# Packed attention and a gated feed-forward in one kernel: two weight loads moved ahead, two output chunks begun within h of batch 0, one packed product on its own

## The chip, the cores and the metric

The kernel runs on one core of a Trainium2 chip. The time is that of the device, in microseconds (us), for one execution; three executions were timed, and their median is the figure. A profile is one further execution, recorded instruction by instruction; it has its own time.

The engines are named as the profile names them: PE is TensorE (matmuls; PEld its weight loads), DVE is VectorE, ACT is ScalarE, POOL is GpSimd (here it mostly issues loads), SP is SyncE (it issues stores and transposes by DMA). Each engine works through its own instructions in order.

## The reference

```python
def sm_attn(qq, kk, vv):
    s = scale * np.matmul(qq, kk.transpose(0, 1, 3, 2))
    s = s - np.max(s, axis=-1, keepdims=True)
    a = np.exp(s)
    a = a / (np.sum(a, axis=-1, keepdims=True) + 1e-09)
    return np.matmul(a, vv)
p_packed = sm_attn(p, k, v)
out = sm_attn(q, p_packed, p_packed)
...
x = np.ascontiguousarray(attn_out.transpose(0, 2, 1, 3)).reshape(B * S, H * D)
...
h = x @ w_in
g = h * np.cos(h)
return (g @ w_out).astype(np.float32)
```

There are 8 batches, 8 heads, 576 tokens and 64 elements a head, with 32 packed queries p a head; w_in is 512 x 2048 and w_out 2048 x 512. All inputs are float32.

## The kernel before

**Stages of a batch b.** `s1(b)`: scores of the packed queries against the keys, and their exp. `a1_pe` or `a1_xbar`: that exp transposed, on TensorE or by a DMA that SP issues. `pp(b)` (line 191): the packed product, exp times values, 48 small matmuls. `pp_T(b)`: its transpose, `ppT`. `ppw(b, n)` (line 213): packed product times quarter n of w_in, into `PPW[b]`; so the second attention and x @ w_in become one product. `s2(b)`, `sums2(b, y)`, `normalise(b)`: exp of the queries' scores against the packed product, their sums, and the normalised weights `a2n`. Then h, in 16 chunks of 128 columns: two or four matmuls of `PPW` and `a2n`, a cosine on ScalarE into `cosT` (a pool of three buffers), and h times cosine on VectorE into `gT`. Last the output: `gT` times `w_out`, in chunks of 128 tokens by 16 matmuls of 512 columns each, copied out of PSUM and stored by SP. 576 tokens are four and a half chunks; the halves of two batches go together in `joint`, chunk 4 of every odd batch.

For batches 0 and 1 a chunk of h has 512 tokens in one PSUM bank (`h_one`, line 295), and `h_half` (line 310) does the last 64 tokens of eight chunks in one bank. Later batches use `h_mm` (line 268), 576 tokens over a pair of banks.

**The filler.** Output matmuls are queued (`set_filler(b)` appends those of batch b) and `fill(n)` issues the next n of them wherever it stands, so that TensorE has work between dependent steps. Those of batch 0 come from `out_first` (line 370), in an order of its own: four chunks are open at once, 0 and 1 in the pool `O` of two banks, 2 and 3 in the pool `psX`. Its tuples are (chunk, up to which of 16).

**PSUM banks.** Beside `O` there are six banks, arranged anew by `banks(kind)`: as three pairs (`psa()` takes them in turn), or as six single ones H0 to H5 (`one()` takes them in turn by `turn[0]`), or with two of them held for `psX`. A bank is written again only after the last reader of what it held.

**The order of the work is written out by hand.** Lines 420 to 517 are the start: the loads, all issued by POOL in the order of the text, attention of batch 0, h of batch 0 (lines 478 to 489), `ppw` of batch 1 for n of 0 to 2 (lines 492 to 497), then the query transposes, `s2`, `sums2` and `normalise` of batch 1. POOL has eight load slots in turn: a load is issued only when the one eight before it has landed. From line 519 on, `slot(s, ...)` runs the 16 chunks of h of batch s. It spreads the output matmuls left in the filler over the chunks by `weight` or `heavy`; `hooks` are (chunk, function) pairs that put other steps in between; with `trail`, the output of batch s itself is appended at chunk 10 and its first `trail` matmuls are issued in the slot; `keep` leaves some for later. `last` is called within chunk 15. In slot 1 the hooks hold the half chunks of batches 0 and 1, the fourth `ppw` of batch 1 and work for batch 2. In slots 2 to 6 the hook is `tiled(s)` (line 540): two `ppw` of batch s and `pp` of batch s+1 in one go, the latter into unused columns of a chunk's bank. Between slots, lines 577 to 610 and 613 to 643 do the attention of the next batches, with fills.

Of the kernel before, what the change touches and what calls it, by code (L numbers as in the profile page):

```python
# [15 lines left out]
def kernel(  # L16
# [143 lines left out]
    def s1(b):  # L160
        ps = scores(lambda r, h, e: P2[r, b, h, :], xT["k", b])
        sm = small.tile([128, 2], FP32, name="sums1")
        for y in range(2):
            ACT.activation(  # L164
                out=a1[b % 2][:, y, :, 0:TP].rearrange("p (e m) x -> p e m x", e=2),
                in_=ps[y][:, :, 0:HS].rearrange("p e (m x) -> p e m x", m=3),
                func=AF.Exp, scale=scale, accum_out=sm[:, y:y + 1])
        sums1[b] = sm
# [22 lines left out]
    def pp(b, eng=V, own=None):  # L191

        ps = own() if own else psa()[:, 0, :]
        for y in range(2):
            for j in range(C):
                c = 2 * (j % 3) + j // 3
                for x in range(4):
                    nc.tensor.matmul(ps[32 * x:32 * x + 32, y * D:(y + 1) * D],  # L198
                                     a1T[b][0:TP, y, j, 32 * x:32 * x + 32],
                                     bf["v", b][:, 2 * x + y, c * D:(c + 1) * D],  # L200
                                     start=(j == 0), stop=(j == C - 1))
        t = pp_sb[b % 2].rearrange("p a d -> p (a d)")
        copy(eng, t[:, 0:2 * D], ps[:, 0:2 * D])
        copy(eng, t[:, 2 * D:3 * D], ps[:, 0:D])

    def pp_T(b, eng=V, own=None):
        ps = own(BF16) if own else psa(BF16)[:, 0, :]
        t = pp_sb[b % 2].rearrange("p a d -> p (a d)")
        for i in range(2):
            nc.tensor.transpose(ps[:, i * 128:(i + 1) * 128], t[:, i * D:i * D + 128], ident)  # L210
        copy(eng, ppT[b % 2].rearrange("p i x n -> p (i x n)"), ps[:, 0:256])

    def ppw(b, n, eng=None, own=None, later=False, cuts=((0, 512),)):
        if b not in PPW:
            PPW[b] = ppw_pool.tile([128, 2, DF], BF16, name="PPW", tag="PPW")
        two = isinstance(eng, tuple)
        if own:
            ps = [own(), own()]
        else:
            t = psa()  # L220
            ps = [t[:, 0, :], t[:, 1, :]]
        for x in range(4):
            for y in range(2):
                r = slice(64 * y, 64 * y + 64)
                nc.tensor.matmul(ps[y][32 * x:32 * x + 32, :], ppT[b % 2][r, 0, x, :],  # L225
                                 w_in_bf[r, x, n * 512:(n + 1) * 512], start=True, stop=True)

        def evacuate(cuts=cuts):
            if own or two:
                for a, z in cuts:  # L230
                    for y in range(2):
                        copy(eng[y] if two else eng, PPW[b][:, y, n * 512 + a:n * 512 + z], ps[y][:, a:z])
            else:
                copy(eng or (V, ACT)[n % 2], PPW[b][:, :, n * 512:(n + 1) * 512], t)
        if later:
            return [lambda c=c: evacuate((c,)) for c in cuts]
        evacuate()
# [131 lines left out]

    def out_first():  # L370

        pss = {}
        for c, fcs in ((0, 4), (1, 4), (2, 4), (3, 4), (0, 8), (1, 8), (2, 8), (3, 8),
                       (2, 12), (3, 12), (2, 16), (3, 16), (0, 16), (1, 16)):
            if c not in pss:
                pss[c] = (O if c < 2 else psum["psX"]).tile([128, DM], FP32, name="ot", tag="ot")
            for fc in range(8 if (c, fcs) in ((0, 16), (1, 16)) else fcs - 4, fcs):
                nc.tensor.matmul(pss[c], gT[0][:, fc, c * 128:(c + 1) * 128], w_out_bf[:, fc, :],  # L378
                                 start=(fc == 0), stop=(fc == NFC - 1))
                if fc == NFC - 1:  # L380
                    store(0, c, pss[c], V if c == 2 else ACT)
                    if c == 3:
                        banks("single")
                        turn[0] = 3
                yield

    filler = []

# [14 lines left out]
    def load_w_in(n):  # L403
        G.dma_start(out=w_in_bf[:, :, n * 512:(n + 1) * 512],
                    in_=moe_w_in.rearrange("(a p) n -> p a n", p=128)[:, :, n * 512:(n + 1) * 512])

    def load_w_out(n):
        G.dma_start(out=w_out_bf[:, n * 4:(n + 1) * 4, :],
                    in_=moe_w_out.rearrange("(a p) n -> p a n", p=128)[:, n * 4:(n + 1) * 4, :])
# [32 lines left out]
    warm(1, None, wz4)  # L442
    pe_T("k", 0, (V, ACT, V))
    s1(0)
    load_w_in(3)
    load("v", 1)
    warm(1, None, wz4, 192)
# [4 lines left out]
    warm(1)  # L452
    pp_T(0)
    pe_T("q", 0, (V, ACT, V))
    load_w_out(0)
    load("q", 1)
    for n in range(1, 4):
        load_w_out(n)
    G.dma_start(out=p_raw[:, 4:, :], in_=p_rows[:, 4:, :])
    load("k", 2)  # L460
# [14 lines left out]
    banks("single")  # L475
    a1_pe(1, own=one)
    recips(1)
    for fc in range(13):
        h_one(0, fc)()()
        if fc in (0, 4, 8):  # L480
            ppw(0, 1 + fc // 4, (ACT, ACT if fc == 8 else V), own=bank)
    c13 = h_one(0, 13)
    pp(1, ACT, own=bank)
    c13()()
    c14 = h_one(0, 14)
    c15 = h_one(0, 15)
    pp_T(1, ACT, own=bank)
    c14()()
    c15()()
    set_filler(0)  # L490
    fill(4)
    for n, at in ((0, 2), (1, 0), (2, 4)):
        turn[0] = at
        if n == 2:
            fill(4)
            ACT.preload_act_table_set(EXP_SET)
        ppw(1, n, (ACT, V), own=one)
    banks("held")
    t = psa(BF16)
    for i in range(2):  # L500
# [10 lines left out]
    sums2(1, 0)  # L511
    fill(2)
    sums2(1, 1)
    fill(9)
    normalise(1)
    ACT.preload_act_table_set(SIN_SET)
    fill(4)

    def slot(s, hooks, keep=0, heavy={}, last=None, trail=0, weight=None):

        left, done = to_do() - keep + trail, 0
        weight = weight or [1 + heavy.get(fc, (0, 0))[0] for fc in range(NFC)]
        for fc in range(NFC):
            rest = h_one(s, fc)() if s == 1 else h_mm(s, fc)
            if fc == NFC - 1 and last:
                last()
            rest()
            if fc == 10 and trail:  # L530
                set_filler(s)
            quota = (left * sum(weight[:fc + 1])) // sum(weight) - done
            done += quota
            behind = min(quota, heavy[fc][1]) if fc in heavy else quota
            fill(quota - behind)
            while hooks and hooks[0][0] == fc:
                hooks.pop(0)[1]()
            fill(behind)
# [19 lines left out]
    def cross(n, b):  # L558
# [1 line left out]

    osb_eng[0] = ACT
    banks("four")
    slot(1, [(5, lambda: h_half(0, 0)), (6, cross("k", 3)), (6, lambda: h_half(0, 1)),
             (7, lambda: ppw(1, 3, (ACT, V), own=one)), (9, cross("q", 2)), (9, lambda: h_half(1, 0)),
             (10, lambda: pack_p(2, 4, one(BF16))), (11, lambda: h_half(1, 1)), (12, tk2),
             (13, lambda: pe_T("k", 2, (None, None, V), (2,), own=one))],
         trail=8, heavy={5: (0, 1), 6: (0, 1), 7: (0, 1), 9: (0, 1), 11: (0, 1)},
         weight=[3, 3, 3, 4, 4, 2, 2, 2, 3, 2, 2, 2, 1, 2, 3, 3])
    banks("pairs")
    ACT.preload_act_table_set(EXP_SET)  # L570
    osb_eng[0] = V
# [36 lines left out]
        load(n, b)  # L608
    fill(9)
    osb_eng[0] = ACT  # L610
    slot(2, [(7, lambda: tiled(2))], 0, {7: (6, 4)}, lambda: pp_T(3, V))

    for s in range(3, B):
        nxt = s + 1 < B
        ACT.preload_act_table_set(EXP_SET)
        osb_eng[0] = V
        if s % 2:
            set_filler(s - 1)
        fill(5)
        s2(s)  # L620
        ppw(s, 0, V)
        fill(8 if nxt else 9)
        if nxt:
            s1(s + 1)
            ppw(s, 1, V)
            a1_xbar(s + 1)
            xbar("q", s + 1)
            recips(s + 1)
            if s + 2 < B:
                xbar("k", s + 2)  # L630
                behind(xT["k", s + 2][0:1, 0, 0:1])
        else:
            for n in range(1, 4):
                ppw(s, n, V)
        fill(4 if nxt else 5)
        sums2(s, 0)
        fill(5)
        sums2(s, 1)
        normalise(s)
        ACT.preload_act_table_set(SIN_SET)  # L640
        fill(13)
        osb_eng[0] = ACT
        for n, b in (("v", s + 2), ("q", s + 2), ("k", s + 3)):
            if b < B:
                load(n, b)
        if nxt:
            slot(s, [(7, lambda: tiled(s))], 0 if s % 2 else 1, {7: (5, 4)}, lambda: pp_T(s + 1, V),
                 7 if s % 2 else 0)
        else:
            slot(s, [], trail=7)  # L650
    fill(1000)
    tail_chunk(B - 1, 4)

# [29 lines left out]
```

## Time and profile before

| what | value |
|---|---|
| median of three runs | 243.86 us (243.74 to 244.26) |
| the profiled execution | 244.22 us, of which the span of the instructions is 242.4 us |
| granted TensorE clock | 0.999 of full |
| matmuls | 2244 |
| idle time of the TensorE rows from 36 to 234 us | 0.6 us |
| w_in's quarters, from issue to landing | 14.3 to 19.7 us, median 17.0 |
| w_out's quarters, from issue to landing | 20.8 to 21.5 us, median 21.1 |
| costliest group: output matmuls, 448 of 128x512 | 114.8 us busy |
| h matmuls of batches 2 to 7, 384 of 128x288 | 62.7 us busy |
| h times cosine on VectorE, 96 of 128x576 | 71.4 us busy, mean 757 ns |

How to read it: a row of the timeline has its start, its length in us, the engine, the line, what it writes and reads, how many instructions were merged into it, and in brackets how long the engine was idle before it and what ended that. Matmuls overlap, so a row's length is longer than the time until the next can start, and idle time in a TensorE row is less than what TensorE really waited. A row of the stretches has, after the stretch and its length, the busy time and count of PE, PEld, DVE, ACT and POOL, then the granted clock, the DMA share and GB/s.

### The profile page before, as it was taken

How to read it: one execution, taken by the hardware profiler on the slowest of the kernel's cores; microseconds unless marked ns; L12 is line 12 of the kernel's file. 1: busy time of each engine (PE TensorE's matmuls, PEld its weight loads, DVE VectorE, ACT ScalarE, POOL GpSimd, SP SyncE). 2: the span in 40 equal slices, each digit the busy share in tenths (PEclk: the TensorE clock that was granted, in tenths of full speed). 3: DMA queues.
4: the chain of work that ended last, by engine and by line, in shares of the span. 5: the costliest groups of instructions: out<-in, count | busy, mean ns of one | idle time of the engine just before them, and what ended most of it. 6: DMA issues, size and time to landing. Idle time of an engine off the chain costs nothing.

```text
span 242.4 us, 5480 instructions
## 1 busy us (share of the span) xinstructions
PE 232.9 (96%) x2244; PEld 126.0 (52%) x2244; DVE 162.8 (67%) x261; ACT 166.5 (69%) x268; POOL 36.2 (15%) x58
## 2 busy tenths in 40 slices
PE   7789899999999999999999999999999999999994
PEld 3454244456445564556546554556456554565453
DVE  3259993688558786687857686777758787877001
ACT  2349899688659778876878677867787683776110
POOL 8522212200300005000500311030100110010000
PEclk9999999999999999999999999999999999999999
DMA  6999999999999999999999999989285101311133
GB/s 96 203 205 206 206 206 225 201 235 201 175 133 162 197 183 166 211 179 179 186 209 225 184 191 208 191 160 213 66 161 119 46 0 46 87 43 46 47 83 87
DMA packets 64376, 37.37 MB, mean 154 GB/s; under 512 B 36864, under 2 KB 59776, under 8 KB 64352
## 3 DMA queue, kind: packets, MB, share of 16 engines
q0 software_dynamic: 23152, 18.75, 51.7%
q1 hardware_dynamic: 40960, 18.16, 37.1%
q8 instruction: 17, 0.28, 0.5%
q10 hardware_dynamic: 240, 0.13, 0.2%
q14 instruction: 7, 0.06, 0.1%
HBM read 37.22 MB, written 9.44 MB: 192 GB/s over the span
## 4 chain that ended last, share of the span: by engine, by line
PE 83%; DMA 8%; DVE 4%; ACT 2%; issue 1%; POOLq 0%
PE ot L365 42%; PE psA L275 17%; PE ot L378 6%; DMA a1T<-a 5%; PE psH L301 4%; DMA kbf<-in_k_dram 3%; PE psA L155 2%; PE psA L225 2%; PE psA L251 2%; PE psA L198 1%; PE ot L348 1%; DVE gT L307 1%; DVE PPW L96 1%; PE psA L128 1%; PE psH L316 1%; DVE a2n L261 1%
## 5 line engine op out<-in xcount | busy, mean ns | idle before, releaser
L365 PE MATMUL ot<-w_out_bf,gT 128*128 128x512 bf16 x448 | 114.8, 379 | 0.0
L282 DVE TENSOR_TENSOR gT<-psA,cosT 128x576 bf16<-128x576 f32 x96 | 71.4, 757 | 16.3 <-ACT cosT L279 15.3
L279 ACT ACTIVATE cosT<-psA 128x576 bf16<-128x576 f32 x96 | 62.4, 652 | 21.3 <-PE psA L275 20.0
L275 PE MATMUL psA<-a2n,PPW 128*128 128x288 bf16 x384 | 62.7, 286 | 0.0
L365 PEld LDWEIGHTS <-gT 128*128 128x128 bf16 x448 | 42.1, 98 | 38.2 <-issue 4.2
L275 PEld LDWEIGHTS <-PPW 128*128 128x128 bf16 x384 | 37.5, 98 | 25.4 <-issue 0.6
L96 DVE CAST PPW<-psA 128x1024 bf16<-128x1024 f32 x19 | 23.0, 1220 | 7.9 <-PE psA L225 7.9
L307 DVE TENSOR_TENSOR gT<-psH,cosT 128x512 bf16<-128x512 f32 x32 | 21.0, 688 | 4.5 <-ACT cosT L306 4.4
L96 DVE COPY osb<-ot 128x512 f32<-128x512 f32 (+2 forms) x18 | 11.7, 649 | 16.1 <-PE ot L348 14.6
L306 ACT ACTIVATE cosT<-psH 128x512 bf16<-128x512 f32 x32 | 18.5, 615 | 4.6 <-PE psH L301 3.5
L94 ACT COPY osb<-ot 128x512 f32<-128x512 f32 (+1 forms) x20 | 11.4, 568 | 14.8 <-PE ot L365 12.2
L261 DVE SCALAR_TENSOR_TENSOR a2n<-a2u,r,lns 128x576 bf16<-128x576 bf16 x16 | 12.4, 815 | 12.4 <-ACT lns L259 12.4
L301 PE MATMUL psH<-a2n,PPW 128*128 128x512 bf16 x64 | 17.7, 380 | 1.0 <-DVE PPW L96 1.0
L378 PE MATMUL ot<-w_out_bf,gT 128*128 128x512 bf16 x64 | 17.8, 380 | 0.1
L286 POOL COPY joint<-gT 128x512 bf16<-128x512 bf16 x12 | 7.3, 616 | 64.6 <-DVE gT L282 64.6
L164 ACT ACTIVATE a<-psA 128x576 bf16<-128x576 f32 x16 | 10.3, 646 | 7.8 <-PE psA L155 7.8
L253 ACT ACTIVATE lns<-psA 128x576 f32<-128x576 f32 x16 | 10.4, 651 | 7.4 <-PE psA L251 6.8
L365 PE MATMUL ot<-w_out_bf,joint 128*128 128x512 bf16 x48 | 14.6, 379 | 0.0
L243 ACT ACTIVATE a2u<-psA,rs 128x576 bf16<-128x576 f32 x16 | 11.0, 737 | 1.4 <-PE psA L155 1.4
L109 POOL COPY gate<-kT 1x1 bf16<-1x1 bf16 x4 | 0.7, 178 | 74.4 <-DMA kT<-kbf 74.4
L301 PEld LDWEIGHTS <-PPW 128*128 128x128 bf16 x64 | 5.8, 98 | 8.3 <-DVE PPW L96 2.0
L259 ACT ACTIVATE lns<-lns 128x576 f32<-128x576 f32 x16 | 10.0, 673 | 0.0
(94 smaller groups left out, 197.0 us busy)
## 6 DMA issues: line engine op xcount, KB each, us to landing
kbf<-in_k_dram POOLq DMA_DIRECT2D x8, 576.0 KB, 14.6
vbf<-in_v_dram POOLq DMA_DIRECT2D x8, 576.0 KB, 8.7
qbf<-in_q_dram POOLq DMA_DIRECT2D x8, 576.0 KB, 11.5
out_dram<-osb SPq DMA_DIRECT2D x24, 192.0 KB, 2.8
out_dram<-osb SPq DMA_DIRECT2D x22, 128.0 KB, 2.5
w_in_bf<-in_moe_w_in_dram POOLq DMA_DIRECT2D x4, 512.0 KB, 17.0
w_out_bf<-in_moe_w_out_dram POOLq DMA_DIRECT2D x4, 512.0 KB, 21.1
out_dram<-osb SPq DMA_DIRECT2D x25, 64.0 KB, 2.7
```

The lines of the kernel that those rows point to most:

```text
L94: ACT.copy(out=out, in_=in_)
L96: eng.tensor_copy(out=out, in_=in_)
L243: ACT.activation(out=a2u[b][:, y].rearrange("p (e x) -> p e x", e=2), in_=ps[y][:, :, 0:HS], func=AF.Exp, scale=rs1[b][:, y:y + 1])
L261: V.scalar_tensor_tensor(out=a2n[b][:, y], in0=a2u[b][:, y], scalar=r1[b][:, y:y + 1], in1=lns[b][:, y], op0=ALU.mult, op1=ALU.mult)
L275: nc.tensor.matmul(ps[:, e, 0:HS], PPW[b][:, y, fc * 128:(fc + 1) * 128], a2n[b][:, y, e * HS:(e + 1) * HS], start=(y == 0), stop=(y == 1))
L279: ACT.activation(out=csv, in_=ps[:, :, 0:HS], func=AF.Sin, bias=PI_HALF)
L282: V.tensor_tensor(out=gT[b][:, fc, :].rearrange("p (e x) -> p e x", e=2), in0=ps[:, :, 0:HS], in1=csv, op=ALU.mult)
L301: nc.tensor.matmul(ps, PPW[b][:, y, fc * 128:(fc + 1) * 128], a2n[b][:, y, 0:512], start=(y == 0), stop=(y == 1))
L306: ACT.activation(out=cs, in_=ps, func=AF.Sin, bias=PI_HALF)
L307: return lambda: V.tensor_tensor(out=gT[b][:, fc, 0:512], in0=ps, in1=cs, op=ALU.mult)
L365: nc.tensor.matmul(ps, w, w_out_bf[:, fc, :], start=(fc == 0), stop=(fc == NFC - 1))
L378: nc.tensor.matmul(pss[c], gT[0][:, fc, c * 128:(c + 1) * 128], w_out_bf[:, fc, :], start=(fc == 0), stop=(fc == NFC - 1))
```

## The change

The first w_out quarter is loaded ahead of w_in's last quarter, the second ahead of batch 1's queries. In h of batch 0 `ppw(0, 3)` moves from behind chunk 8 to behind chunk 11, both half chunks of batch 0 move in from slot 1, and output chunks 0 and 1 begin: one matmul behind each of chunks 8 to 11 and four behind the first half chunk. `pp(1)` and `pp_T(1)` take single banks in place of `O`. All four `ppw(1, n)` follow, without `turn[0]` being set. One more fill follows the table load, and the last long fill has 10 in place of 9. Chunks 0 and 1 of `out_first` are taken to eight at once, then 2 and 3. In slot 1 the moved hooks go, the weights are new and 12 output matmuls of batch 1 are issued in place of 8. In slot 2 the two `ppw` stay at chunk 7 and `pp(3)` goes to chunk 10, into a bank pair of its own, and 6 output matmuls of batch 2 are issued in the slot. `slot` loses `keep`; a batch's output is appended at chunk 7 of its own slot always, with trails of 13 (odd slots from 3 on) and 5 (even ones), and is no longer appended ahead of the odd slots.

```diff
-        pss = {}
-        for c, fcs in ((0, 4), (1, 4), (2, 4), (3, 4), (0, 8), (1, 8), (2, 8), (3, 8),
-                       (2, 12), (3, 12), (2, 16), (3, 16), (0, 16), (1, 16)):
+        pss, at = {}, [0] * 4
+        for c, to in ((0, 4), (1, 4), (0, 8), (1, 8), (2, 8), (3, 8), (2, 16), (3, 16), (0, 16), (1, 16)):
...
-                        turn[0] = 3
+                        turn[0] = 4
...
     s1(0)
+    load_w_out(0)
     load_w_in(3)
     load("v", 1)
...
-    load_w_out(0)
+    load_w_out(1)
     load("q", 1)
-    for n in range(1, 4):
+    for n in range(2, 4):
         load_w_out(n)
...
-    for fc in range(13):
+    set_filler(0)
+    for fc in range(12):
         h_one(0, fc)()()
-        if fc in (0, 4, 8):
-            ppw(0, 1 + fc // 4, (ACT, ACT if fc == 8 else V), own=bank)
+        if fc in (0, 4):
+            ppw(0, 1 + fc // 4, (ACT, V), own=bank)
+        if fc >= 8:
+            fill(1)
+    for evac in ppw(0, 3, (ACT, V), own=one, later=True, cuts=((0, 128), (128, 512))):
+        evac()
+    h_half(0, 0)
+    fill(4)
+    h_one(0, 12)()()
     c13 = h_one(0, 13)
-    pp(1, ACT, own=bank)
+    pp(1, ACT, own=one)
     c13()()
     c14 = h_one(0, 14)
     c15 = h_one(0, 15)
-    pp_T(1, ACT, own=bank)
+    pp_T(1, ACT, own=one)
     c14()()
     c15()()
-    set_filler(0)
-    fill(4)
-    for n, at in ((0, 2), (1, 0), (2, 4)):
-        turn[0] = at
+    h_half(0, 1)
+    for n in range(4):
         if n == 2:
             fill(4)
-            ACT.preload_act_table_set(EXP_SET)
         ppw(1, n, (ACT, V), own=one)
+    ACT.preload_act_table_set(EXP_SET)
+    fill(4)
...
-    fill(9)
+    fill(10)
     normalise(1)
...
-        left, done = to_do() - keep + trail, 0
+        left, done = to_do() + trail, 0
...
-            if fc == 10 and trail:
+            if fc == 7:
                 set_filler(s)
...
-    slot(1, [(5, lambda: h_half(0, 0)), (6, cross("k", 3)), (6, lambda: h_half(0, 1)),
-             (7, lambda: ppw(1, 3, (ACT, V), own=one)), (9, cross("q", 2)), (9, lambda: h_half(1, 0)),
-             (10, lambda: pack_p(2, 4, one(BF16))), (11, lambda: h_half(1, 1)), (12, tk2),
+    slot(1, [(5, lambda: h_half(1, 0)), (6, cross("k", 3)), (7, lambda: h_half(1, 1)), (9, cross("q", 2)),
+             (10, lambda: pack_p(2, 4, one(BF16))), (12, tk2),
              (13, lambda: pe_T("k", 2, (None, None, V), (2,), own=one))],
-         trail=8, heavy={5: (0, 1), 6: (0, 1), 7: (0, 1), 9: (0, 1), 11: (0, 1)},
-         weight=[3, 3, 3, 4, 4, 2, 2, 2, 3, 2, 2, 2, 1, 2, 3, 3])
+         12, {5: (0, 1), 7: (0, 1)}, weight=[4, 4, 3, 3, 3, 1, 2, 1, 2, 2, 2, 2, 1, 1, 2, 3])
...
-    slot(2, [(7, lambda: tiled(2))], 0, {7: (6, 4)}, lambda: pp_T(3, V))
+    slot(2, [(7, lambda: ppw(2, 2, ACT)), (7, lambda: ppw(2, 3, V)), (10, lambda: pp(3))], 6, {7: (4, 3), 10: (2, 2)},
+         lambda: pp_T(3, V))
...
-        if s % 2:
-            set_filler(s - 1)
         fill(5)
...
-            slot(s, [(7, lambda: tiled(s))], 0 if s % 2 else 1, {7: (5, 4)}, lambda: pp_T(s + 1, V),
-                 7 if s % 2 else 0)
+            slot(s, [(7, lambda: tiled(s))], 13 if s % 2 else 5, {7: (5, 4)}, lambda: pp_T(s + 1, V))
         else:
-            slot(s, [], trail=7)
+            slot(s, [], 13)
```

More of the change, by code (lines that the diff above doesn't have):

```diff
@@ L370, in out_first @@
     def out_first():
-        pss = {}
-        for c, fcs in ((0, 4), (1, 4), (2, 4), (3, 4), (0, 8), (1, 8), (2, 8), (3, 8),
-                       (2, 12), (3, 12), (2, 16), (3, 16), (0, 16), (1, 16)):
+        pss, at = {}, [0] * 4
+        for c, to in ((0, 4), (1, 4), (0, 8), (1, 8), (2, 8), (3, 8), (2, 16), (3, 16), (0, 16), (1, 16)):
             if c not in pss:
                 pss[c] = (O if c < 2 else psum["psX"]).tile([128, DM], FP32, name="ot", tag="ot")
-            for fc in range(8 if (c, fcs) in ((0, 16), (1, 16)) else fcs - 4, fcs):
+            for fc in range(at[c], to):
                 nc.tensor.matmul(pss[c], gT[0][:, fc, c * 128:(c + 1) * 128], w_out_bf[:, fc, :],
@@ L383, in out_first @@
                         banks("single")
-                        turn[0] = 3
+                        turn[0] = 4
                 yield
+            at[c] = to
     filler = []
@@ L517, with slot @@
     fill(4)
-    def slot(s, hooks, keep=0, heavy={}, last=None, trail=0, weight=None):
-        left, done = to_do() - keep + trail, 0
+    def slot(s, hooks, trail, heavy={}, last=None, weight=None):
+        left, done = to_do() + trail, 0
         weight = weight or [1 + heavy.get(fc, (0, 0))[0] for fc in range(NFC)]
```

## The prediction

> **What bounds the kernel now.** I read the page's busy table first, then the busy time of each engine in stretches of 6 us, then the list of waits, then the timeline of the two places the change touches.
>
> ```profile
> PE 232.9 (96%) x2244; PEld 126.0 (52%) x2244; DVE 162.8 (67%) x261; ACT 166.5 (69%) x268; POOL 36.2 (15%) x58
> ...
> 18.00:24.00 6.00, 5.82 (x73) 2.98 (x72) 5.89 (x14) 5.96 (x12) 1.48 (x2) 1.00 1.24 206
> 24.00:30.00 6.00, 4.99 (x34) 1.62 (x33) 6.00 (x11) 5.33 (x12) 1.81 (x2) 1.00 1.28 205
> 30.00:36.00 6.00, 5.95 (x102) 2.61 (x102) 5.60 (x11) 5.86 (x13) 0.78 (x1) 1.00 1.28 206
> 36.00:42.00 6.00, 6.00 (x57) 3.04 (x55) 2.04 (x3) 5.56 (x10) 1.53 (x2) 1.00 1.24 219
> ...
> PE psA L198 <- DMA a1T<-a: 0.5, 1, 0.5
> ```
>
> TensorE bounds the whole: 96%, and from 36 us on every stretch is full but a few tenths. Both kernels issue the same matmuls, so the time can change only by the time in which TensorE waits or drains. The second to fourth rows are the exception: from 18 to 36 us, h of batch 0, VectorE is full (5.89, 6.00, 5.60 of 6) and ScalarE nearly. Here VectorE and ScalarE pace, and this is where the change puts more work. The last row is the second place.
>
> ```profile
> 27.75 0.39 PE L301 MATMUL psH<-a2n,PPW 128*128 128x512 bf16 x1 [0.64 <-DVE PPW L96]
> 30.75 0.55 PE L198 MATMUL ot<-vbf,a1T 96*32 96x64 bf16 x48
> 31.24 1.04 PE L301 MATMUL psH<-a2n,PPW 128*128 128x512 bf16 x4
> 31.76 0.43 ACT L94 CAST pp_sb<-ot 128x128 bf16<-128x128 f32 x2
> 32.01 0.68 ACT L306 ACTIVATE cosT<-psH 128x512 bf16<-128x512 f32 x1
> 32.51 0.45 ACT L94 COPY ppT<-ot 128x256 bf16<-128x256 bf16 x1
> 32.53 1.04 PE L378 MATMUL ot<-w_out_bf,gT 128*128 128x512 bf16 x4
> 32.78 1.17 ACT L306 ACTIVATE cosT<-psH 128x512 bf16<-128x512 f32 x2
> 33.50 0.74 PE L225 MATMUL psH<-w_in_bf,ppT 64*32 64x512 bf16 x16
> 34.17 1.04 PE L378 MATMUL ot<-w_out_bf,gT 128*128 128x512 bf16 x4
> 37.50 0.72 PE L155 MATMUL psA<-qT,ppT 64*32 64x288 bf16 x16
> ...
> 82.40 0.62 PE L225 MATMUL psA<-w_in_bf,ppT 64*32 64x512 bf16 x16
> 83.48 0.56 PE L198 MATMUL psA<-vbf,a1T 96*32 96x64 bf16 x48 [0.46 <-DMA a1T<-a]
> 91.06 0.27 PE L210 MATMUL psA<-ident,pp_sb 128*128 128x128 bf16 x2
> ```
>
> A row's length holds the tail of its last matmul, so I count from start to start. Thirteen 128x512 matmuls start at 39.95 and the next work at 42.75: 0.2155 us each. A 64-row block of 8 (L225) takes 0.34 (52.01 to 52.35) and 0.09 ahead of it (51.70 to 52.01 for one 512 matmul); a pair of blocks 0.67 (33.50 to 34.17). The 48 small matmuls of L198 take 0.49 (30.75 to 31.24). A half chunk of h (L316, 16 matmuls) takes 0.47 (49.26 to 49.73).
>
> **The loads.** All go through POOL's one queue; w_in's third and last quarters are seen landed at 24.78 and 27.37 (the idle ends of POOL's next issues), the first w_out quarter at 32.5 (it holds the 32.53 matmul) and batch 1's queries at 35.5. So a weight quarter takes about 2.6. With the new order: w_out quarter 0 at 27.4, w_in's last at 30.0, v of batch 1 at 32.5 (the same bytes are then ahead of it as were ahead of w_out 0), queries at 38.0; the other two w_out quarters and all behind stay. Needed, by the steps below, at 27.96, 30.2, 32.9 and 39.8: margins 0.6, 0.2, 0.4 and 1.8. I cost the new order at nothing; every us of further lateness of the first three would stand on TensorE. SP's queue now has chunk 0's store ahead of the transposes of batch 3's keys; those are used at 68 us, so nothing.
>
> **h of batch 0, step by step.** The last common TensorE instruction is at 27.75. After it, in the new order: 4 out matmuls and chunks 9 to 11, 10 x 0.2155 from 27.96: 30.12. ppw(0,3), 0.09 + 0.34: 30.55. h_half, 0.47: 31.02. Four out matmuls: 31.88. Chunks 12 and 13, with 0.05 for the cast of ppw(0,3) on VectorE (gT of chunk 5 starts at 27.60, each next 0.60 later, so chunk 11's ends and the two cuts are done at 32.5): 32.8. pp(1), 0.09 + 0.49: 33.4. Chunks 14, 15: 34.25. pp_T, about 0.2 (estimate, from 0.06 a transpose and the drain): 34.45. h_half: 34.9. Then ppw(1,0), whose ppT comes from ScalarE.
>
> ScalarE's order is now: cos 12, the two pp_sb casts, cos 13, ppT, cos 14, cos 15, cos of the half chunk. pp's last result is there at 33.45; pp_sb starts at 33.5, cos 13 0.25 behind it (31.76 to 32.01), 33.75 to 34.43. ppT waits for pp_T's result, 34.6, although cos 14's input is long there; cos 14 starts 0.27 behind it (32.51 to 32.78), 34.9 to 35.55; cos 15 0.49 later, to 36.1. VectorE follows: gT 14 from 35.6 to 36.3, gT 15 from 36.2 to 36.9. ppw(1,0) starts at 35.1, when ppT is copied, and is issued by 35.35.
>
> Here is the new wait. The six psH banks are taken in turn; by the new count chunk 14 has H2, chunk 15 H3, and ppw(1,0) takes H0, H1, so ppw(1,1) takes H2 and H3 and cannot write its second bank until gT 15 is done. Before, `turn[0]` was set by hand so that ppw(1,0) and (1,1) took the banks of chunks 10 to 13. TensorE is in order: behind this wait stand 4 out matmuls, ppw(1,2), (1,3), the query transposes and s2(1). It resumes at 36.95, a wait of 1.55. From there: rest of the block 37.27, 4 matmuls 38.13, 0.09 + 0.67 for the pair of blocks 38.9, 4 matmuls 39.76, query transposes 1.02 (35.53 to 36.54) 40.8, 4 matmuls 41.65, 0.09: s2(1) starts at 41.75 against 37.50. ScalarE: the four casts end at 39.9, table load 1.28, qT copy 0.80: 41.95, as close behind s2's start as before (37.75). From s2(1) to slot 1 the same work and one more out matmul: slot 1 starts at 42.75 + 4.25 + 0.22 = 47.2.
>
> What is then done that was done later before: 9 out matmuls 1.94, two half chunks 0.94, ppw(1,3) 0.43, together 3.31. Slot 1 was full before and has less work for every engine now. The stage costs 47.2 - 42.75 - 3.31 = **+1.15 us**. Bounds: if gT 14 and 15 came 0.7 earlier (cos at its lone 0.60, ppT not in the way) +0.45; if a load is late by 0.5, +1.65.
>
> **Slot 2.** TensorE's ppw block there starts at 82.40 and pp(3) only at 83.48, held by the transpose of a1 (batch 3); the block itself takes 0.56 (108.99 to 109.55 in slot 3), so the hold is 0.52. Now three chunks (0.49 each) and some eight out matmuls stand between: 3.2 later in the slot, and the transpose moves by at most the 2 us by which s1(3) moves, so the hold goes: -0.52. The separate pp(3) pays the change of array shape once more, 0.09 ahead: +0.09. pp_T(3), 91.06, was held 0.28 for its bank pair (chunk 13's gT ends at 91.02); there is one out matmul more between chunk 13 and it: -0.2. Sum **-0.63**; between 0 (pp's bank pair holds the ring of three) and -0.8. The Trainium skill, "TensorEngine Tiling (Array Packing)", Tiling Modes, says that a change of tiling mode drains TensorE, which speaks against parting the blocks; without that rule and its row the sum here would be -0.72.
>
> **Slots 3 to 7.** Counted from the quotas, each slot still issues 36, 37, 37, 37 and 35 out matmuls; six more are done ahead. TensorE has nothing there but drains of about 0.2 a block, and pace is held by TensorE: 0, at most +0.5 if a chunk's copy lands in a bad place.
>
> **Sum:** +1.15 - 0.63 = +0.5. The profiled execution (244.22, span 242.4) would become 244.7; the runs' median is 0.36 below it, so 243.86 + 0.5 = **244.4**.
>
> **Rivals.**
> - *The bank wait is short* (other side, faster): if gT 15 comes early enough that ppw(1,1) hardly waits, the stage costs 1.15 - 1.55 = -0.4, the sum is -1.0: 242.8. For it: VectorE alone, at 0.60 an operation from 31.2, could be through gT 15 by about 35.7. Against: ScalarE's order, which holds cos 14 behind ppT. It decides from a wait under 1.05. Chance 0.17.
> - *Half of it*: a wait of 0.6 to 1.5 with the full slot 2 gain, within 0.2%: about 243.9. Chance 0.23.
> - *Slot 2 gives nothing*, because pp(3)'s own bank pair stalls the ring of three pairs: 243.86 + 1.15 = 245.0. Against: pp_sb's casts take only 0.42 of VectorE (84.12). Chance 0.15.
> - *A load is late*: w_in's last quarter or v by 0.5 to 1 past its margin: 245.1. For it: the load queue is full to 50 us. Chance 0.10.
> - *The clock drops* in the wait. The trace has a gap from 6.56 to 8.22 (1.66) with a granted clock of 1.00 in that window, so no. The Trainium skill, "TensorE: Matmul & The Clock Gate", Part 1, has it halve after an idle window of some 3.4 us; by that a window at half pace would cost 1.7, an estimate from the page: 246. Chance 0.02.
> - The forecast, slower by about 0.5: 0.33.
>
> A measurement of this kernel tells about 0.2% (0.5 us) from no change; the forecast lies on that line, and the forecast's own spread and the next three rivals fall on its slower side. Faster 0.17, same 0.23, slower 0.60. Likeliest case alone: 244.2 to 244.8; with the rivals, leaving out the far end of the first and the last: 243.2 to 245.4.
>
> **What would show it.** Right: a TensorE wait of 1 to 2 us on gT just ahead of L225 near 36 us, slot 1 starting near 47.2, no hold at pp(3). Wrong: no such wait, a wait for a load in L377 near 28 us, or new idle time past 95 us.

## The result, and the profile after

The changed kernel takes 247.68 us (median of four runs, 247.37 to 247.96) against 243.93 us for the kernel before in the same runs (243.74 to 244.26). The ratio is 1.0152, with a 95% interval of 1.0134 to 1.0170: slower by 3.75 us, where +0.5 was forecast and 245.4 was the upper end of the range. The profiled execution took 247.37 us with a span of 245.6 us, against 242.4 before.

In the list of waits of the changed kernel (columns: engine, what it was to write, line, what it waited for; then us in all, how often, the longest), the wait for batch 3's transpose is gone, as forecast. Four kinds are new (the third is at 22.46 us, ahead of all that was moved):

```profile
PE ot L365 <- DVE gT L282: 1.5, 3, 0.5
...
PE psH L225 <- DVE gT L307: 1.0, 3, 0.6
...
PE ot L225 <- DMA w_in_bf<-in_moe_w_in_dram: 0.2, 1, 0.2
...
PE psA L275 <- ACT PPW L94: 0.2, 1, 0.2
```

The stretches from 18 to 42 us, beside those of the kernel before in the prediction:

```profile
18.00:24.00 6.00, 5.62 (x72) 2.85 (x70) 5.89 (x15) 5.96 (x13) 1.66 (x3) 1.00 1.24 206
24.00:30.00 6.00, 5.17 (x30) 1.79 (x27) 6.00 (x12) 5.33 (x11) 1.81 (x2) 1.00 1.26 206
30.00:36.00 6.00, 5.41 (x111) 2.95 (x111) 4.91 (x9) 4.62 (x13) 0.78 (x1) 1.00 1.29 205
36.00:42.00 6.00, 5.51 (x74) 2.59 (x75) 4.85 (x8) 4.69 (x7) 0.91 (x2) 1.00 1.25 220
```

TensorE, full from 30 us on before (5.95 and 6.00), now has half a microsecond free in each of the last two. VectorE has fallen from 5.60 to 4.91 and ScalarE from 5.86 to 4.62 in the third: neither is the bound by volume, so it is the order of dependent steps that makes TensorE wait. The granted clock is 1.00 throughout.

The timeline of TensorE in the first stage:

```profile
35.23 0.41 PE L225 MATMUL psH<-w_in_bf,ppT 64*32 64x512 bf16 x8 [0.18 <-DVE gT L307]
36.27 0.37 PE L225 MATMUL psH<-w_in_bf,ppT 64*32 64x512 bf16 x1 [0.62 <-DVE gT L307]
36.87 0.41 PE L225 MATMUL psH<-w_in_bf,ppT 64*32 64x512 bf16 x7 [0.23 <-DVE gT L307]
37.21 1.04 PE L377 MATMUL ot<-w_out_bf,gT 128*128 128x512 bf16 x4
...
41.59 0.71 PE L155 MATMUL psA<-qT,ppT 64*32 64x288 bf16 x16
...
47.05 0.59 PE L301 MATMUL psH<-a2n,PPW 128*128 128x512 bf16 x2
```

The first row is `ppw(1,0)`, the next two `ppw(1,1)`, one block cut in two by its two banks. The first bank comes free with chunk 14's `gT` and the second with chunk 15's. Two blocks of 0.34 back to back would end at 35.91; the output matmuls behind them start at 37.21, so the waits cost 1.30. Slot 1 starts at 47.05.

Slot 2, from its first matmul at 77.56 (before: 75.45) to the end of its last chunk at 93.21 (before: 90.77):

```profile
84.38 0.63 PE L225 MATMUL psA<-w_in_bf,ppT 64*32 64x512 bf16 x16
84.94 0.82 PE L365 MATMUL ot<-w_out_bf,joint 128*128 128x512 bf16 x3
85.93 0.67 PE L275 MATMUL psA<-a2n,PPW 128*128 128x288 bf16 x4 [0.17 <-ACT PPW L94]
...
88.06 0.59 PE L365 MATMUL ot<-w_out_bf,joint 128*128 128x512 bf16 x2
88.58 0.55 PE L198 MATMUL psA<-vbf,a1T 96*32 96x64 bf16 x48
89.07 0.61 PE L365 MATMUL ot<-w_out_bf,joint 128*128 128x512 bf16 x2
```

`pp(3)` (88.58) is not held: the two matmuls ahead of it end at 88.06 + 2 x 0.2155 = 88.49, and 0.09 is what the prediction read for a change of array shape. But chunk 8 (85.93) now stands 0.34 behind the end of the three matmuls ahead of it (84.94 + 0.65 = 85.59). It needs quarter 2 of `PPW`, which ScalarE is still copying:

```profile
84.86 1.01 ACT L94 CAST PPW<-psA 128x1024 bf16<-128x1024 f32 x1 [0.59 <-PE psA L225]
```

In the kernel before, `pp(3)` (0.5 us) and four output matmuls, not three, stood between that block and chunk 8 and covered this copy.

Behind slot 3, the changed kernel:

```profile
119.19 0.65 PE L275 MATMUL psA<-a2n,PPW 128*128 128x288 bf16 x4
...
119.64 0.76 DVE L282 TENSOR_TENSOR gT<-psA,cosT 128x576 bf16<-128x576 f32 x1 [0.16 <-ACT cosT L279]
119.68 0.28 PE L210 MATMUL psA<-ident,pp_sb 128*128 128x128 bf16 x2
...
119.79 1.05 PE L365 MATMUL ot<-w_out_bf,gT 128*128 128x512 bf16 x4
119.88 0.65 ACT L279 ACTIVATE cosT<-psA 128x576 bf16<-128x576 f32 x1 [0.27 <-PE psA L275]
...
120.45 0.10 PEld L365 LDWEIGHTS <-gT 128*128 128x128 bf16 x1 [0.35 <-DVE gT L282]
...
120.56 0.76 DVE L282 TENSOR_TENSOR gT<-psA,cosT 128x576 bf16<-128x576 f32 x1
...
121.37 0.33 PEld L365 LDWEIGHTS <-gT 128*128 128x128 bf16 x3 [0.83 <-DVE gT L282]
121.38 0.82 PE L365 MATMUL ot<-w_out_bf,gT 128*128 128x512 bf16 x3 [0.53 <-DVE gT L282]
```

TensorE is done with slot 3's last chunk at 119.68. VectorE finishes `gT` of that chunk only at 120.56 + 0.76 = 121.32, because ScalarE's cosine (119.88 to 120.53) comes in between. An output chunk is made of 16 matmuls, its pieces 0 to 15, and piece n needs `gT` of chunk n of h. With a trail of 13 the slot has used up pieces 0 to 12 of batch 3's first output chunk, so the `fill(5)` behind it asks for pieces 13, 14 and 15 at once. The four matmuls at 119.79 (the slot's last two, then 13 and 14) end at 120.65, the next starts at 121.38: 0.73 lost. The same gap stands behind slots 5 and 7, where it comes to 0.73 and 0.62. The kernel before, at the same place:

```profile
117.46 1.67 PE L365 MATMUL ot<-w_out_bf,gT 128*128 128x512 bf16 x7
...
118.23 0.76 DVE L282 TENSOR_TENSOR gT<-psA,cosT 128x576 bf16<-128x576 f32 x1
...
119.06 0.44 PE L155 MATMUL psA<-qT,ppT 64*32 64x288 bf16 x16
```

The last chunk's `gT` ends no sooner behind its matmuls (117.35 to 118.99, 1.64 again), but nobody asks for it. By the quotas of `slot`, with a trail of 7 the seven matmuls are pieces 5 to 11 of the same output chunk, all long ready; pieces 12 to 15 come only behind `s2` and `ppw`.

### The profile page after: what moved, and what is told of

Same layout as the page of the kernel before. It is cut to its first block, busy times and chain, and to the rows that moved or that the text cites. A ratio compares the mean times of both kernels' runs of the same rounds, so it can differ in the third digit from the quotient of the medians.

```text
span 245.6 us, 5480 instructions
## 1 busy us (share of the span) xinstructions
PE 233.3 (95%) x2244; PEld 125.5 (51%) x2244; DVE 164.1 (67%) x263; ACT 165.8 (68%) x268; POOL 36.9 (15%) x58
## 4 chain that ended last, share of the span: by engine, by line
PE 81%; DMA 12%; DVE 3%; ACT 2%; issue 1%; POOL 0%; POOLq 0%
PE ot L365 42%; PE psA L275 19%; DMA vbf<-in_v_dram 12%; PE ot L377 5%; PE psH L301 3%; PE psA L225 2%; PE psA L155 2%; DVE gT L282 2%; PE ot L348 1%; PE psA L251 1%; PE psA L198 1%; DVE gT L307 1%; ACT cosT L279 1%; ACT cosT L306 0%; PE psH L128 0%
## 5 line engine op out<-in xcount | busy, mean ns | idle before, releaser
L365 PE MATMUL ot<-w_out_bf,gT 128*128 128x512 bf16 x448 | 116.6, 379 | 1.6 <-DVE gT L282 1.5
L279 ACT ACTIVATE cosT<-psA 128x576 bf16<-128x576 f32 x96 | 62.4, 653 | 22.7 <-PE psA L275 21.7
L365 PEld LDWEIGHTS <-gT 128*128 128x128 bf16 x448 | 41.9, 98 | 39.8 <-issue 4.2
L301 PE MATMUL psH<-a2n,PPW 128*128 128x512 bf16 x64 | 18.2, 380 | 0.8 <-DVE PPW L96 0.8
L365 PE MATMUL ot<-w_out_bf,joint 128*128 128x512 bf16 x48 | 14.3, 380 | 0.0
```

The lines of the kernel that those rows point to most:

```text
L279: ACT.activation(out=csv, in_=ps[:, :, 0:HS], func=AF.Sin, bias=PI_HALF)
L301: nc.tensor.matmul(ps, PPW[b][:, y, fc * 128:(fc + 1) * 128], a2n[b][:, y, 0:512], start=(y == 0), stop=(y == 1))
L365: nc.tensor.matmul(ps, w, w_out_bf[:, fc, :], start=(fc == 0), stop=(fc == NFC - 1))
```

## The experiments

Every kernel's median is given beside that of the kernel before in the runs that it shares. In several of these traces some 35 matmul records are missing, so lengths are read from start to start.

### The trails of the odd slots

e1: the changed kernel with the trails cut to 9.

```diff
-    ..., 13 if s % 2 else 5, {7: (5, 4)}, ...
+    ..., 9 if s % 2 else 5, {7: (5, 4)}, ...
-            slot(s, [], 13)
+            slot(s, [], 9)
```

> The changed kernel with 9 in place of 13 of its own output matmuls issued in the odd slots 3, 5 and 7. Theory A (the output matmuls that come right behind such a slot need gT of chunks 13 to 15, which VectorE finishes only about 1.6 us after TensorE leaves the slot; the profile has 0.71, 0.71 and 0.62 us of such waits): with four fewer they stand behind five matmuls and s2, the three waits go, about 2.0 us less than the changed kernel, 245.6 to 245.9. Theory B (VectorE paces these slots and a wait removed here only comes back in the slot): no change, 247.7.

Measured: 245.63 us against 243.76, ratio 1.0075 (1.0062 to 1.0088): 2.05 less than the changed kernel's 247.68, and L365 no longer waits for `gT` in its list of waits.

e2: the kernel before with the trails raised to 13 and nothing else.

```diff
-                 7 if s % 2 else 0)
+                 13 if s % 2 else 0)
-            slot(s, [], trail=7)
+            slot(s, [], trail=13)
```

> The kernel before, with 13 in place of 7 own output matmuls in slots 3, 5 and 7 and nothing else. Theory A (the trail alone makes the three waits): about +2.0 us on the kernel before, 245.9, with three waits of 0.6 to 0.7 us on gT. Theory B (the waits need the late start that the change's first stage brings): 243.9. The prediction had priced this at 0, at most +0.5.

Measured: 245.63 against 243.76, ratio 1.0093 (1.0059 to 1.0127): +1.87 by the medians, while one of its six runs took 248.23 and lifts the ratio. Its list of waits has the same entry as the changed kernel's, and its timeline a gap at the same place behind slot 3:

```profile
PE ot L365 <- DVE gT L282: 1.1, 3, 0.5
```

```profile
118.18 1.03 PE L365 MATMUL ot<-w_out_bf,gT 128*128 128x512 bf16 x4
119.55 0.60 PE L365 MATMUL ot<-w_out_bf,gT 128*128 128x512 bf16 x2 [0.34 <-DVE gT L282]
```

Four matmuls from 118.18 end at 119.04, so 0.51 is lost here and as much behind slot 5, against 0.73 in the changed kernel. Three such gaps do not make up the whole 1.87; where the rest stands was not followed. Taken away from the one and put into the other, the trails give 2.05 and 1.9 us: over half of the change's loss.

### Slot 2

e3: the kernel before with slot 2's hooks of the change, and the trail left at 0.

```diff
-    slot(2, [(7, lambda: tiled(2))], 0, {7: (6, 4)}, lambda: pp_T(3, V))
+    slot(2, [(7, lambda: ppw(2, 2, ACT)), (7, lambda: ppw(2, 3, V)), (10, lambda: pp(3))], 0, {7: (4, 3), 10: (2, 2)},
+         lambda: pp_T(3, V))
```

> The kernel before with slot 2's hooks alone changed: the two ppw at chunk 7, pp(3) at chunk 10 in a bank pair of its own, no own output matmuls. The prediction priced this at -0.63: 243.3. Theory A now (the hold of 0.52 at pp(3) goes, but chunk 8 needs the ppw quarter that ScalarE copies for 1.0 us, and with only three matmuls between it waits 0.3, and pp_T stays held): -0.1 to -0.3, 243.7. Rival (the ring of bank pairs stalls): slower than before.

Not as expected: 244.16 (11 runs) against 243.76 (17 runs), ratio 1.0015 (1.0007 to 1.0024), so it is slower by 0.4. Its TensorE timeline:

```profile
82.23 0.62 PE L225 MATMUL psA<-w_in_bf,ppT 64*32 64x512 bf16 x16
82.79 0.82 PE L365 MATMUL ot<-w_out_bf,joint 128*128 128x512 bf16 x3
83.90 0.66 PE L275 MATMUL psA<-a2n,PPW 128*128 128x288 bf16 x4 [0.28 <-ACT PPW L94]
...
86.33 0.56 PE L198 MATMUL psA<-vbf,a1T 96*32 96x64 bf16 x48
```

Chunk 8 waits for ScalarE's copy here too: the three matmuls end at 83.44, so 0.46 is lost. Its list of waits names no wait for a bank, so the ring of bank pairs is not what stalls. Either the hold that this edit was to remove is not in every execution of the kernel before, or the edit loses what it gains. So:

e11: the kernel before, profiled once more.

> The kernel before, once more, for its second slot. Theory (the hold of 0.5 us at batch 3's transposes, on which the prediction's gain in slot 2 rests, belonged to the one profiled execution): slot 2 takes 14.8 us from its first matmul to the last, with no wait above 0.1 us at the transposes. Rival (the hold belongs to the kernel): 15.3 us and a wait of 0.5 there.

```profile
82.39 0.63 PE L225 MATMUL psA<-w_in_bf,ppT 64*32 64x512 bf16 x16
82.95 0.56 PE L198 MATMUL psA<-vbf,a1T 96*32 96x64 bf16 x48
83.66 0.81 PE L365 MATMUL ot<-w_out_bf,joint 128*128 128x512 bf16 x3 [0.16 <-issue]
84.31 0.65 PE L275 MATMUL psA<-a2n,PPW 128*128 128x288 bf16 x4
```

`pp(3)` follows its block 0.56 behind, with no hold, and chunk 8 waits for nobody. Slot 2 runs from 75.44 to 90.24, 14.80 us, where the first profile had 75.45 to 90.77, 15.32. This execution took 243.68 us with a span of 241.9. Slot 2 with `tiled(2)` shows no hold in e2, e4, e6, e7, e8, e9 and e10 either. The hold of 0.52 belonged to the one execution that was profiled first. e3's slot takes 75.50 to 90.79, 15.29: 0.49 more than e11's. The changed kernel's takes 15.65 with two output matmuls more (0.43), so 0.42 more.

### The loads

e4: the kernel before with the new order of loads only.

```diff
+    load_w_out(0)
     load_w_in(3)
...
-    load_w_out(0)
+    load_w_out(1)
     load("q", 1)
-    for n in range(1, 4):
+    for n in range(2, 4):
         load_w_out(n)
```

> The kernel before with the new order of the loads alone. The prediction: 0, the margins hold. Theory A: -0.1 to -0.2 (the first output matmul of batch 0 no longer waits 0.2 for w_out), 243.6 to 243.8. Rival: w_in's last quarter and v of batch 1 come too late, +0.3 or more. Its profile is also one more look at pp(3) in slot 2, which this kernel runs as before: theory A there is that the hold of 0.5 in the profile of the kernel before belonged to that execution (the transpose of a1 landed late in it), since the kernel before with another trail ran slot 2 with no hold, 82.35 to 82.91.

Not as expected: 246.21 against 243.80, ratio 1.0096 (1.0081 to 1.0110), +2.4. The three loads that were pushed back all hold TensorE:

```profile
29.53 0.41 PE L225 MATMUL ot<-w_in_bf,ppT 64*32 64x512 bf16 x8 [1.48 <-DMA w_in_bf<-in_moe_w_in_dram]
...
32.44 0.56 PE L198 MATMUL ot<-vbf,a1T 96*32 96x64 bf16 x48 [0.24 <-DMA vbf<-in_v_dram]
...
37.90 0.85 PE L128 MATMUL psA<-ident,qbf 96*128 96x96 bf16 x16 [1.09 <-DMA qbf<-in_q_dram]
```

In the changed kernel the work stands in another order: `ppw(0,3)` starts at 30.14, `pp(1)` at 32.95, the query transposes at 39.60, and its list of waits names none for these loads. But the room is small: batch 1's v landed 21.7 us behind its issue at 11.26, at about 32.9, right where `pp(1)` starts, and in e6, which has the same loads and the same order of work up to there, `pp(1)` waits 0.24 for it (33.18). The new loads are nearly free, and only together with the new order of work.

### The first stage alone

e6: the changed kernel with slots 1 to 7 put back: slot 1's trail at 8, slot 2 with `tiled(2)` and no trail, the later trails at 7 and 0.

```diff
-         12, {5: (0, 1), 7: (0, 1)}, weight=[4, 4, 3, 3, 3, 1, 2, 1, 2, 2, 2, 2, 1, 1, 2, 3])
+          8, {5: (0, 1), 7: (0, 1)}, weight=[4, 4, 3, 3, 3, 1, 2, 1, 2, 2, 2, 2, 1, 1, 2, 3])
...
-            ..., 13 if s % 2 else 5, ...
+            ..., 7 if s % 2 else 0, ...
```

> The changed kernel with slots 1 to 7 put back: own output matmuls 8 in slot 1, 0 in slot 2, 7 and 0 from slot 3 on, and slot 2 with tiled(2); loads, h of batch 0 and what moved into it stay changed. Theory A (the first stage costs 1.0 by the two profiles, slots 3, 5, 7 cost 2.0 together, the wait behind slot 1 costs 0.3, and pp(3) alone costs 0.4): 243.8 + 1.0 = 244.8. The prediction had +1.15 for this stage: 244.9. Rival (the first stage hurts later stages too, by transposes and loads that start later): 245.3 or more.

Not as expected: 246.02 against 243.80, ratio 1.0089 (1.0075 to 1.0103), +2.2. Its timeline holds a wait that the changed kernel does not have:

```profile
50.09 0.59 PE L377 MATMUL ot<-w_out_bf,gT 128*128 128x512 bf16 x2
51.66 0.59 PE L301 MATMUL psH<-a2n,PPW 128*128 128x512 bf16 x2 [0.98 <-DVE gT L307]
```

The two matmuls end at 50.52, so 1.14 is lost. The likely reason is an artefact: with fewer output matmuls to spread, the 48th of batch 0, at which `out_first` sets the banks to single ones, falls one chunk later, and chunk 3 is given a bank whose `gT` is not done. e9 tests that: the same kernel, with weights that keep the 48th where it was.

```diff
-          8, ..., weight=[4, 4, 3, 3, 3, 1, 2, 1, 2, 2, 2, 2, 1, 1, 2, 3])
+          8, ..., weight=[4, 4, 3, 3, 2, 1, 2, 1, 2, 2, 1, 2, 1, 1, 1, 2])
```

> The first stage alone in its changed order, as in e6, with slot 1's weights rewritten so that its count of 48 falls behind chunk 1 and chunk 3 has a bank of its own. Theory (e6 holds an artefact of 1.1 us, the wait at 50.30 to 51.66 for chunk 2's bank): the wait is gone and the kernel takes 244.8 to 244.9 us, which is 243.8 plus the 1.0 that the start of slot 1 lost. Rival (the first stage alone costs 2.2, and the wait only moves to another place of slot 1): 246.0 us again.

Measured: 245.01 against 243.80, ratio 1.0047 (1.0034 to 1.0060), with no such wait in slot 1. The first stage alone costs 1.2 us.

### The bank wait

e5: the changed kernel with the four output matmuls that stood behind `ppw(1,1)` put ahead of it. e7: the same edit on e6.

```diff
     for n in range(4):
-        if n == 2:
+        if n == 1:
             fill(4)
```

> The changed kernel with the four output matmuls that stand between ppw(1,1) and ppw(1,2) moved ahead of ppw(1,1), into the wait for the bank of chunk 15. Theory A (the wait of about 1.2 us there is idle time that those four, 0.86, can fill, and ScalarE's casts and table load end earlier with it): about -0.6 us, 247.1. Rival (ScalarE's four casts, the table load and the query copy end as late as before, and s2(1) waits for them instead): 247.7, with a wait for ScalarE ahead of s2(1).

> The same as the run before it, with four output matmuls moved from behind ppw(1,1) to ahead of it. Theory A: the wait for chunk 15's bank was 1.1 us of TensorE with nothing in it; four matmuls fill 0.86: 244.8 - 0.8 = 244.0, within 0.2 of the kernel before. Rival: s2(1) is held by ScalarE's table load and query copy, half of it is given back: 244.4.

Measured: e5 246.68 against 243.76, ratio 1.0122 (1.0103 to 1.0142), 1.0 less than the changed kernel by the medians and 0.7 by the ratios; e7 245.29 against 243.80, ratio 1.0058 (1.0044 to 1.0071), 0.73 less than e6. That e7 lies above both of its expected times is e6's other wait, 0.98 for `gT` in slot 1, which e7 and e8 still have.

e8: eight ahead of `ppw(1,1)`, none behind `ppw(1,3)`.

```diff
-        if n == 2:
-            fill(4)
+        if n == 1:
+            fill(8)
...
-    fill(4)
```

> The same with all eight output matmuls ahead of ppw(1,1): the four behind ppw(1,3) move there too. Theory A: nothing of the wait is left (1.73 of matmuls into 1.5), the casts start as soon as the banks are free, and the table load with them: 243.7 to 243.9, as the kernel before. Rival: TensorE then has nothing for the time in which VectorE and ScalarE copy the four ppw, and waits ahead of the query transposes instead: 244.4 or more.

Measured: 245.83 against 243.80, ratio 1.0079 (1.0066 to 1.0092), 0.54 more than e7. The bank wait is covered, but nothing stands any longer between `ppw(1,3)` and the queries, and the loss comes back in three places:

```profile
38.73 0.85 PE L128 MATMUL psA<-ident,qbf 96*128 96x96 bf16 x16 [0.40 <-DMA qbf<-in_q_dram]
...
41.47 0.42 PE L155 MATMUL psA<-qT,ppT 64*32 64x288 bf16 x10 [0.45 <-ACT qT L94]
...
47.32 0.38 PE L301 MATMUL psH<-a2n,PPW 128*128 128x512 bf16 x1 [0.30 <-DVE a2n L261]
```

e10: e9 with the edit of e7.

> e9 with the first four of PPW's out matmuls ahead of chunk 1's product of quarter 1, as in e7. Theory (these four cover 0.7 of the bank wait): 244.0 to 244.2 us, within 0.2 per cent of before. Rival (the wait of e6 was no artefact): 245.3 us.

Measured: 244.18 (11 runs) against 243.80, ratio 1.0017 (1.0008 to 1.0026). With its bank wait covered, the whole new first stage costs 0.4 us. Its timeline in place of the wait:

```profile
35.17 0.41 PE L225 MATMUL psH<-w_in_bf,ppT 64*32 64x512 bf16 x8 [0.19 <-DVE gT L307]
35.51 1.04 PE L377 MATMUL ot<-w_out_bf,gT 128*128 128x512 bf16 x4
36.48 0.73 PE L225 MATMUL psH<-w_in_bf,ppT 64*32 64x512 bf16 x9
37.40 0.41 PE L225 MATMUL psH<-w_in_bf,ppT 64*32 64x512 bf16 x8 [0.19 <-DVE joint L321]
37.99 0.41 PE L225 MATMUL psH<-w_in_bf,ppT 64*32 64x512 bf16 x7 [0.19 <-DVE PPW L96]
```

Two shorter waits for banks now stand in `ppw(1,2)` and `ppw(1,3)`, with no output matmuls left between these blocks.

### Both repairs together

e12: the changed kernel with the edits of e1 and e5.

> The changed kernel with the trails of slots 3, 5 and 7 at 9 and with four out matmuls ahead of chunk 1's product of quarter 1, the edits of e1 and e5 together. Theory (the wait for the bank of gT near 36 us and the waits behind the odd slots are two separate losses, and TensorE never gives time back in between): the gains add, 245.63 less 0.8 = 244.8 to 244.9 us, and what is left over before, 1.0, is the rest of the first stage, behind slot 1 and slot 2. Rival (what the first stage gains is lost again further on, in slot 2 or behind slot 1, where VectorE or a transfer sets the pace): 245.4 to 245.6 us.

Measured: 244.78 against 243.75, ratio 1.0048 (1.0035 to 1.0062). The two gains add: 0.85 below e1. What is left over before, 1.03, is close to e10's 0.38, slot 2's 0.4 and some 0.3 behind slot 1 together. No kernel of these beats the kernel before; of those with the new first stage, e10 comes nearest.

## Why the prediction was wrong

| term | forecast | measured |
|---|---|---|
| first stage | +1.15 | +1.0 (trace: slot 1 starts 4.30 later with 3.31 more done); +1.2 (e9) |
| behind slot 1 | not counted | about +0.3 (trace only) |
| slot 2 | -0.63 | +0.4 (e3) |
| slots 3 to 7 | 0 | +1.9 (e2), +2.05 (e1) |
| loads | 0 | no wait named in the changed kernel; 0.24 in e6 |
| sum | +0.5 | +3.6 to +3.95; the kernels themselves: +3.75 |

**The step that failed** is the one headed "Slots 3 to 7": "TensorE has nothing there but drains of about 0.2 a block, and pace is held by TensorE: 0, at most +0.5 if a chunk's copy lands in a bad place." It counted how many output matmuls each slot issues and not which ones. That the count is unchanged says nothing of the trail, which went from 7 to 13. Inside the slot the pieces 0 to 12 are all ready; the fill behind the slot is where the trail decides, since it goes on with piece 13 when VectorE has just finished `gT` 13, and `gT` 15 ends 1.64 us behind the chunk's matmuls (119.68 to 121.32). The rows for it were in the profile before: `gT` of slot 3's last chunk started at 118.23 there, 0.9 behind the end of that chunk on TensorE. The traces place the loss: from its first matmul to the next slot's, slot 3 takes 27.02 us and slot 5 27.25 in the changed kernel, against 26.29 and 26.51 in e11, while slots 4 and 6 take the same in both. The sum was thus too small by 2.0, and 244.4 + 2.0 is outside the range. Without this loss the kernel still takes 245.63 (e1), just above the range's end of 245.4; slot 2's wrong sign is the next part. No rival had this mechanism, though new idle time past 95 us was a named sign of being wrong.

**Slot 2** had the wrong sign, for two reasons. The gain of 0.52 rested on a hold seen in one execution, which e11 and seven other traces of the same slot do not show. And the step costed what stood ahead of `pp(3)` in its new place, but not what it had hidden in its old one: chunk 8's wait for the copy of `PPW`, 0.46 in e3 and 0.34 in the changed kernel. The 0.09 for the second change of array shape was right (88.49 to 88.58): here the Trainium skill's page "TensorEngine Tiling (Array Packing)", Tiling Modes, which says that a change of mode drains TensorE, agrees with the trace. Of the 0.2 at `pp_T(3)` half came: its transposes start 0.18 behind the last chunk in the changed kernel (93.21 to 93.39), 0.28 in e11; in e3, without the own output matmuls, still 0.29. The rival "slot 2 gives nothing" had the sign nearer, by another cause.

**The first stage** was right in mechanism, place and size. The wait for the banks of chunks 14 and 15 was forecast to end at 36.95, and its last part ended at 36.87 (1.30 in all, 1.55 forecast); `s2(1)` started at 41.59 (forecast 41.75) and slot 1 at 47.05 (forecast 47.2). The edit of e5, e7 and e10 shows that the wait is the cause: four matmuls put into it bring 0.7 to 0.85 of 1.2 back (e5's medians say 1.0). The rival by which the wait is short falls: 1.30 is above its limit of 1.05. The rival "half of it" had the wait within its 0.6 to 1.5, but not slot 2's gain.

**The loads** were forecast to land with margins of 0.2 to 1.8 in the new order. e4, which consumes them in the old order, shows their landing by the ends of the waits: 29.5, 32.4 and 37.9, against 30.0, 32.5 and 38.0 forecast. In the changed kernel v came at about 32.9 and the queries, 21.5 behind their issue at 17.37, at about 38.9: 0.4 and 0.9 later than forecast, so v's margin of 0.4 was used up, while the queries' larger one held. The rival of a late load, by 0.5 to 1 past its margin, falls; a lateness of 0.24 was seen (e6).

**The clock** stayed at 1.00 in the stretches that hold the 1.30 us of waits (30 to 42 us), so that rival falls for waits of this length. The gap that the prediction reads as 1.66 was shorter: a matmul still ran in it, and the idle time ahead of 8.22 is 1.06. The longest idle time of TensorE in the lists of waits is 1.9 us (e2, ahead of 8.15, with a granted clock of 1.00). No run here shows an idle time of some 3.4 us against which to hold the rule of the Trainium skill, "TensorE: Matmul & The Clock Gate", Part 1.

**Behind slot 1** the 0.3 is read from the trace and was not tried by itself: with 12 of batch 1's pieces issued in the slot, a weight load at 64.84 waits for `gT`, and the scores behind seven matmuls start at 65.16, 0.39 behind the 64.77 at which these end; in the kernel before they start 0.10 behind theirs. By these rows it is the mechanism of the trails once more.

## What to carry to other kernels

Moving filler work between stages is judged by which pieces stand at each join, not by how many: where a producer trails by 1.6 us, as here (matmul, ScalarE, VectorE), its last pieces must not be asked for within that time. What kept the join dense, with a trail of 7 or 9, is that pieces long ready were left for it, and the last ones came behind further steps. Before a step is moved, ask what it hid in its old place; before a hold is counted as a gain, look for it in more than one execution.

## What was not expected of the hardware

The same kernel's wait for a transpose made by DMA was 0.52 us in one execution and nothing in the next, and the spans differed by just that (242.4 and 241.9), while the times of 15 runs of it lie within 243.6 to 244.3. That transpose was issued at 70.1 in both and landed 13.3 us later in the one and 10.6 in the other. A term of half a microsecond at a DMA's landing is within what one execution differs from another.
